# Two scatters in place of one for the last token tile of a two-tile slot

## The chip, the cores and the metric

The kernel runs on one core of a Trainium2 chip. The metric is the device time of one execution in microseconds (us): the median of several runs. The profile shows one execution instruction by instruction. Its engines are PE (TensorE: matmuls), DVE (VectorE), ACT (ScalarE), POOL (GpSimd, which also issues the indirect DMAs) and SP (SyncE, which issues the plain loads).

## The reference

Attention with a soft cap on the scores is followed by a mixture of experts in which every token goes to exactly one of eight experts. The change lies in the second part, and there in the line that writes `out[mask]`.

```python
def _moe_ref(x, modality_id, w_gate, modality_bias, w1, w2):
    # x (3584, 768), w1 (8, 768, 1024), w2 (8, 1024, 768)
    logits = x @ w_gate + modality_bias[modality_id]
    e_idx = np.argmax(logits, axis=1)
    ...
    for e in range(E):
        mask = e_idx == e
        h = np.maximum(x[mask] @ w1[e], 0.0)
        out[mask] = gate_w[mask, None] * (h @ w2[e])
```

## The kernel before, in words

The tokens of an expert are worked on in slots of up to 384 rows, that is three token tiles of 128 rows (`TW = 3`). A plan that the kernel makes on the chip says which expert and which rows each slot has. Eight full slots run first. Then a branch picks one of four ends (`ENDS`, L57 of the program) by the plan; on this input it is the first, `(2, 2, 0)`: a slot of two tiles, a second slot of two tiles, and up to 32 left-over rows of one expert ("few"), whose matmuls are placed among those of the second two-tile slot. Below, "slot A" and "slot B" are these two slots and "few" is the third part.

A slot is `run_slot`: `ffn1` makes the hidden layer, with matmuls of L1103, L1104 and L1107 into `ph`, a relu on ACT (`hh`, L1113) and the rest of the split on DVE (`hl`, L1114). `ffn2` makes the output. For each token tile `t` it runs 48 matmuls of L1139 into two PSUM tiles `py`, one for each half of the 768 columns; tile 0 mixes the two halves, every later tile finishes half 0 before it starts half 1. ACT scales each finished half by the gate weight into the SBUF tile `ot` (L1144), and when both are there POOL issues one indirect DMA (L1145) that scatters 128 rows of 3072 bytes to `out` by the row numbers in `mt`. Few has an `ot` of its own, `of` (L1268), and a scatter of its own (L1269) of 128 rows of 768 bytes, since four quarters of a row lie on four groups of partitions.

Weights come as FP32 through SP loads (L107) into four `raw` buffers, shared in turn; ACT casts each to its high part (L990, `ah`, `bh`), DVE subtracts to get the low part (L991, `al`, `bl`), and with that the buffer is free for the load four places on. The rows of x for the next slot are gathered by POOL (L970), scaled and transposed on DVE.

The order on each engine is that of the program as the scheduler leaves it; every engine works through its queue in order, so an instruction that waits holds up those behind it. Waits are put in where two instructions touch the same tile or tensor. Each scatter of the tiles writes the tensor `out`, so each waits for the landing of the one before it, unless the two are declared independent, which only few's scatter was. The line L1306 is the branch that leaves an end, L1554 the close of the program, where all engines meet.

Of the kernel before, what the change touches and what calls it, by code (L numbers as in the profile page):

```python
# [42 lines left out]
I32 = mybir.dt.int32  # L43
AF = mybir.ActivationFunctionType
ALU = mybir.AluOpType
# [7 lines left out]
NT, DM, FF, E, NM = B * S, H * D, 1024, 8, 2  # L53
# [8 lines left out]
TW = W // 128  # L62
# [23 lines left out]
class Program:  # L86
# [8 lines left out]
    def pin(self, inst):  # L95
        return self.tc.keep_in_program_order(inst)
# [243 lines left out]
    def slots(self, pool, ps, early):  # L340
# [78 lines left out]
        if early:  # L419
            pair = tile("pair", [128, E])  # L420
            V.scalar_tensor_tensor(pair, rem, 128.0, sm, op0=ALU.is_gt, op1=ALU.mult)
            two = tile("two", [128, 1])
            V.tensor_reduce(two, pair, axis=AX.X, op=ALU.add)
            V.tensor_scalar(two, two, NB, float(FIXED + 2), op0=ALU.add, op1=ALU.is_le)
            first = tile("first1", [128, 1])
            V.scalar_tensor_tensor(first, NB, float(FIXED), two, op0=ALU.is_le, op1=ALU.mult)
            other = tile("other", [128, 1])
            V.scalar_tensor_tensor(other, NB, float(FIXED + 1), two, op0=ALU.is_le, op1=ALU.mult)
            V.tensor_tensor(other, other, first, op=ALU.subtract)
            V.tensor_scalar(begin, total, float(FIXED + 2), 2.0, op0=ALU.is_gt, op1=ALU.add)  # L430
            V.tensor_tensor(begin, begin, other, op=ALU.mult)
            V.tensor_tensor(end, begin, other, op=ALU.add)
            V.scalar_tensor_tensor(end, first, 2.0, end, op0=ALU.mult, op1=ALU.add)
            few = tile("few", [128, 1])
            V.scalar_tensor_tensor(pair, rem, float(FEW), sm, op0=ALU.is_gt, op1=ALU.mult)
            V.tensor_reduce(few, pair, axis=AX.X, op=ALU.add)
            V.tensor_scalar(few, few, NB, float(FIXED + 2), op0=ALU.add, op1=ALU.is_le)
            V.tensor_tensor(few, few, first, op=ALU.mult)
            V.tensor_tensor(end, end, few, op=ALU.subtract)
            V.scalar_tensor_tensor(begin, first, 3.0, begin, op0=ALU.mult, op1=ALU.add)  # L440

            fits = tile("fits", [128, 1])
            V.tensor_scalar(fits, begin, float(FIXED), total, op0=ALU.add, op1=ALU.is_ge)
            V.tensor_tensor(end, end, fits, op=ALU.mult)
            V.memset(begin, float(FIXED))
        else:
            V.memset(plan[:, 1:], 0.0)
# [673 lines left out]
    def ffn2(self, mt, n, at={}, pin=lambda inst: inst):  # L1121

        nc = self.nc
        for t in range(n):
            ot = self.lp.tile([128, C * 256], F32, name="ot", tag="late", bufs=3)[:, :DM]
            rows = slice(t * 128, (t + 1) * 128)
            steps = [[(half, f, a, c) for f in range(FC) for a, c in ((0, 0), (0, 1), (1, 0))] for half in range(2)]
            if t == 0:
                late = [(0, f, 0, 1) for f in range(FC - 3, FC)]
                steps = [[step for step in steps[0] if step not in late] + steps[1][:9] + late, steps[1][9:]]  # L1130
            py, left = [None, None], [3 * FC, 3 * FC]
            for half, f, a, c in steps[0] + steps[1]:
                if a == c == 0 and (2 * t + half, f) in at:
                    at[2 * t + half, f]()
                if py[half] is None:
                    py[half] = self.ps_y.tile([128, 512], F32, name="py")
                cs = slice(half * HALF, (half + 1) * HALF)
                left[half] -= 1
                self.latest["tensor"] = nc.tensor.matmul(  # L1139
                    py[half][:, :HALF], self.h[a][:, f, rows], self.w2s[f][c][:, cs],  # L1140
                    start=left[half] == 3 * FC - 1, stop=left[half] == 0,
                ).ins
                if left[half] == 0:
                    self.latest["scalar"] = pin(nc.scalar.mul(ot[:, cs], py[half][:, :HALF], mt[:, t, 1:2])).ins  # L1144
            self.last_out = nc.gpsimd.indirect_dma_start(  # L1145
                self.out, bass.IndirectOffsetOnAxis(ap=mt.bitcast(I32)[:, t, 0:1], axis=0), ot, None,
                bounds_check=NT - 1, oob_is_err=False,
            )
            self.latest["gpsimd"] = self.last_out.ins

    def run_slot(self, cur, n, ahead=None, between=(), mark=None):
# [111 lines left out]
    def run_few(self, e, rows):  # L1263

        nc, (mt, index) = self.nc, rows
        self.few2(e, (2, 3, 4, 5), True)
        ot = self.small_tile("of")[:, :QC]
        nc.scalar.mul(ot, self.yf[:, :QC], mt[:, 1:2])  # L1268
        put = nc.gpsimd.indirect_dma_start(  # L1269
            self.out.rearrange("n (g d) -> (n g) d", g=4), bass.IndirectOffsetOnAxis(ap=index[:, 0:1], axis=0), ot, None,  # L1270
            bounds_check=4 * NT - 1, oob_is_err=False,
        )
        self.tc.declare_no_dep(put.ins, self.last_out.ins, reason="every token is in one slot of the plan")

    def run_slots(self, cur, order, table):

# [33 lines left out]

    def end(self, end, at, ahead):

        self.last_sp = None
        tiles = ENDS[end]
        for i, n in enumerate(tiles):
            later = (lambda: ahead(FIXED + i + 1, tiles[i + 1])) if i + 1 < len(tiles) else None
            if n:
                at = self.run_slot(at, n, later)
            else:
                self.run_few(*at[:2])  # L1320

    def finish(self, which, end, cur, ahead):

        tc = self.tc
        if end == len(ENDS):
            self.tail()
            return
        with tc.If(which == end + 1, preferred_fallthrough_block=False) as branch:
            self.end(end, cur, ahead)
        with branch.Else():  # L1330
            self.finish(which, end + 1, cur, ahead)
# [122 lines left out]
    def build(self):  # L1454
        tc, nc = self.tc, self.nc
        with ExitStack() as st:
            self.nstage, self.latest = 2, {}
            self.cpool = st.enter_context(tc.tile_pool(name="cpool", bufs=1))
            dram = st.enter_context(tc.tile_pool(name="dram", bufs=1, space=DRAM))
            self.plani = self.cpool.tile([1, 3], I32, name="plani")  # L1460
            with ExitStack() as sa:
                self.up = sa.enter_context(tc.tile_pool(name="up", bufs=1))
                first = self.first = self.load_kq(0, parts=2)
                with tc.tile_pool(name="ps_w", bufs=1, space=PSUM) as ps_w:
                    self.constants(self.cpool, dram)
                    self.warm(ps_w, 13, 256)
                big = nc.values_load(self.flag[0:1, 0:1], min_val=0, max_val=1)
                with tc.If(big != 0, preferred_fallthrough_block=False) as branch:
                    self.general()
                    self.tail(fresh=True)  # L1470
                with branch.Else():
                    with ExitStack() as sb:
                        self.moe_pools(sb)
                        self.small = "xT1"
                        rt = sb.enter_context(tc.tile_pool(name="rt", bufs=1))
                        early, late = self.attention(first, rt)
                        self.moe_pools2(sb)

                        table = []

                        def order():
                            table.append(self.slots(rt, self.ps_r, True))
                            self.meta = next(table[0])

                        w2 = lambda at, *ks: (at, lambda: self.load_w2(early[0], self.raws, range(*ks)))
                        self.run_slots(early, (
                            *late, (3, order), w2(3, 0, 4), *(w2(f, f, f + 1) for f in range(4, FC)),
                        ), table)
# [70 lines left out]
```

## Time and profile before

| | |
|---|---|
| median of 3 runs | 801.45 us (801.19 to 802.93) |
| profiled execution, its own time | 802.65 us |
| its span, first to last instruction | 800.80 us |
| PE busy | 791.1 us, 99% of the span |
| DVE, ACT, POOL busy | 555.2, 513.0, 306.5 us |
| scatters of tiles, L1145 | 28, mean 1137 ns on POOL |

The page gives busy times and shares over the whole span. PE is busy for 99% of it, so what there is to read are PE's few gaps and the time behind its last matmul. A row of the timeline has the start in us, the length in us, the engine, the line, the operation and its tiles, with the count at its end (several instructions in a row are merged), and in brackets how long the engine had been idle before it and what released it. A letter q behind an engine (POOLq, SPq) is its queue: waits, moves, DMA issues and the closing of the program. The view of stretches has the busy time of each engine in each stretch, then the granted clock as a share, the mean busy share of the 16 DMA engines and the GB/s moved. In the view of the DMA queues q1 carries the loads of SP and q0 the DMAs of POOL.

### The profile page before, as it was taken

Reading aid. Unit: us, or ns where it says so; the run is one execution under the profiler, and the core shown is the slowest. Engines: PE = TensorE matmul, PEld = TensorE weight load, DVE = VectorE, ACT = ScalarE, POOL = GpSimd, SP = SyncE. Lnnn points to the kernel's source line nnn. Section 1 sums busy time; section 2 is a strip of 40 time slices with the busy share of each in tenths; the row PEclk is TensorE's granted clock in tenths of the full one; section 3 lists DMA queues with packets and bytes.
Section 4 is the critical chain, followed back from the end, with each engine's and each line's share of the span. In section 5 each row is a group of like instructions: output and inputs, shape, how many; then the busy total and the mean of one; then the engine's idle time right before and its main releaser. Section 6 shows DMA issues by size and latency. Waiting matters only on the chain. (4 is left out here: it accounts for less than half of the span.)

```text
span 800.8 us, 14596 instructions
## 1 busy us (share of the span) xinstructions
PE 791.1 (99%) x5272; PEld 624.2 (78%) x5272; DVE 555.2 (69%) x1086; ACT 513.0 (64%) x598; POOL 306.5 (38%) x382
## 2 busy tenths in 40 slices
PE   8999999999999999999999999999999999999997
PEld 4444454444445445999999999999999999999986
DVE  6889898999999999966383753737437374356820
ACT  7999999999999998365252542535425354245611
POOL 2122423232324145457565273542745417014201
PEclk9999999999999999999999999999999999999999
DMA  6475464746556444497366382563825638248654
GB/s 214 148 237 193 146 192 125 212 149 197 173 167 204 137 155 151 112 338 245 106 202 233 108 278 84 182 231 112 275 76 179 229 112 265 70 141 263 204 219 166
DMA packets 55939, 144.77 MB, mean 181 GB/s; under 512 B 11567, under 2 KB 19585, under 8 KB 55858
## 3 DMA queue, kind: packets, MB, share of 16 engines
q1 hardware_dynamic: 40960, 109.42, 41.0%
q0 software_dynamic: 14752, 34.33, 14.1%
q8 instruction: 43, 0.70, 0.4%
q14 instruction: 38, 0.31, 0.1%
q10 hardware_dynamic: 146, 0.00, 0.0%
HBM read 114.91 MB, written 24.34 MB: 174 GB/s over the span
## 5 line engine op out<-in xcount | busy, mean ns | idle before, releaser
L1103 PE MATMUL ph<-x,ah 128*128 128x384 f32 (+1 forms) x480 | 156.5, 326 | 1.3 <-DVE hl L1114 1.3
L1104 PE MATMUL ph<-x,ah 128*128 128x384 f32 (+1 forms) x480 | 155.9, 325 | 0.0
L1107 PE MATMUL ph<-x,al 128*128 128x384 f32 (+1 forms) x480 | 155.9, 325 | 0.0
L1139 PE MATMUL py<-bh,hl 128*128 128x384 f32 x448 | 149.9, 335 | 0.9 <-DVE hl L1114 0.9
L1139 PE MATMUL py<-bh,hh 128*128 128x384 f32 x448 | 150.3, 336 | 0.0
L1139 PE MATMUL py<-bl,hh 128*128 128x384 f32 x448 | 146.5, 334 | 0.0
L970 POOL DMA_INDIRECT xg<-xd,at x93 | 116.2, 1249 | 50.4 <-issue 23.5
L702 POOL DMA_DIRECT2D xd<-xs x96 | 61.2, 645 | 174.4 <-DVE xs L696 170.0
L557 ACT ACTIVATE pt<-sc,isc 128x896 f32<-128x896 f32 x129 | 120.6, 1009 | 5.7 <-PE sc L553 2.9
L991 DVE TENSOR_TENSOR bl<-raw,bh 128x768 fp32r<-128x768 f32 x80 | 74.3, 956 | 70.5 <-ACT bh L990 56.6
L560 ACT ACTIVATE pt<-pt,cabs 128x2688 f32<-128x2688 f32 x48 | 122.0, 2541 | 0.8
L602 PE MATMUL xT<-pt,va 128*64 128x448 f32 x576 | 118.8, 548 | 1.1 <-ACT pt L560 1.1
L1113 ACT ACTIVATE hh<-ph 128x384 fp32r<-128x384 f32 (+1 forms) x80 | 37.3, 469 | 124.5 <-PE ph L1107 119.7
L1114 DVE SCALAR_TENSOR_TENSOR hl<-ph,hh 128x384 fp32r<-128x384 f32 (+1 forms) x80 | 41.8, 527 | 105.9 <-ACT hh L1113 105.8
L1103 PEld LDWEIGHTS ph<-x,ah 128*128 128x128 f32 x480 | 90.1, 188 | 1.7 <-DVE hl L1114 1.7
L1145 POOL DMA_INDIRECT out_dram<-ot,mt x28 | 31.8, 1137 | 152.4 <-ACT ot L1144 141.2
L1104 PEld LDWEIGHTS ph<-x,ah 128*128 128x128 f32 x480 | 90.1, 188 | 0.0
L1107 PEld LDWEIGHTS ph<-x,al 128*128 128x128 f32 x480 | 90.1, 188 | 0.0
L990 ACT CAST bh<-raw 128x768 fp32r<-128x768 f32 x80 | 64.3, 834 | 32.3 <-DMA raw<-in_w_dram 25.6
L1139 PEld LDWEIGHTS py<-bh,hl 128*128 128x128 f32 x448 | 84.1, 188 | 1.2 <-DVE hl L1114 1.2
L1139 PEld LDWEIGHTS py<-bh,hh 128*128 128x128 f32 x448 | 84.1, 188 | 1.2 <-issue 0.7
L1139 PEld LDWEIGHTS py<-bl,hh 128*128 128x128 f32 x448 | 83.8, 188 | 0.0
(217 smaller groups left out, 1307.3 us busy)
## 6 DMA issues: line engine op xcount, KB each, us to landing
raw<-in_w_dram SPq DMA_DIRECT2D x86, 384.0 KB, 4.0
raw<-in_w_dram SPq DMA_DIRECT2D x60, 512.0 KB, 5.3
kq<-in_kq_dram SPq DMA_DIRECT2D x47, 448.0 KB, 4.6
va<-in_v_dram SPq DMA_DIRECT2D x24, 448.0 KB, 6.1
xd<-xs POOLq DMA_DIRECT2D x96, 112.0 KB, 3.8
cg<-gl SPq DMA_DIRECT2D x22, 224.0 KB, 2.2
raw<-in_w_dram SPq DMA_DIRECT2D x12, 256.0 KB, 3.8
mapd<-pre SPq DMA_DIRECT2D x4, 480.0 KB, 5.2
```

Source lines behind the costliest of these rows:

```text
L557: pin(nc.scalar.activation(out, sc[:, :, :S], AF.Tanh, scale=scale))
L560: pin(nc.scalar.activation(x, x, AF.Exp, scale=self.cabs))
L602: pin(pe.matmul(xT[j * D : (j + 1) * D, :S], va[:, u * D : (u + 1) * D], quads[q]["pt"][t, i][:, j], start=t == i == 0, stop=t == 1 and i ...
L702: (nc.gpsimd.dma_start(self.xd[b * S : (b + 1) * S, a, r * 64 : (r + 1) * 64].rearrange("(n p) f -> p n f", p=32), d["out"][a * 32 : (a + ...
L970: got = self.nc.gpsimd.indirect_dma_start(self.xg[:, c], None, self.xd.rearrange("n a x -> (n a) x"), bass.IndirectOffsetOnAxis(ap=at[:, c ...
L990: a = self.nc.scalar.copy(hi, raw)
L991: b = self.nc.vector.tensor_tensor(lo, raw, hi, op=ALU.subtract)
L1103: nc.tensor.matmul(ph[:, :w], hi[:, fs], self.x[k][:, 0, :w], start=first, stop=False)
L1104: nc.tensor.matmul(ph[:, :w], hi[:, fs], self.x[k][:, 1, :w], start=False, stop=False)
L1107: nc.tensor.matmul(ph[:, :w], lo[:, fs], self.x[k][:, 0, :w], start=False, stop=last)
L1114: self.latest["vector"] = nc.vector.scalar_tensor_tensor(hl[:, f, :w], acc, 0.0, hh[:, f, :w], op0=ALU.max, op1=ALU.subtract).ins
L1139: self.latest["tensor"] = nc.tensor.matmul(py[half][:, :HALF], self.h[a][:, f, rows], self.w2s[f][c][:, cs], start=left[half] == 3 * FC - ...
```

## The change

In `ffn2`, the last tile of a slot with fewer than three tiles (`n < TW and t == n - 1`) is written by two scatters of 128 rows of 1536 bytes, one for each half of the columns. `out` is seen for this as a tensor with twice as many rows of half the length, so each half needs row numbers of its own, 2 x row and 2 x row + 1: POOL makes them with two small `tensor_scalar` into a tile `twice`, of which there is one buffer. All other tiles keep one scatter. The scatters of an end are collected in `self.puts` and each is declared independent of those before it in the same end.

```diff
@@ ffn2
             rows = slice(t * 128, (t + 1) * 128)
+            where, parts = mt.bitcast(I32)[:, t, 0:1], 1
+            if n < TW and t == n - 1:
+                parts = 2
+                both = self.lp.tile([128, parts], I32, name="twice")
+                for h in range(parts):
+                    nc.gpsimd.tensor_scalar(both[:, h : h + 1], where, float(parts), float(h), op0=ALU.mult, op1=ALU.add)
+                where = both
...
-            self.last_out = nc.gpsimd.indirect_dma_start(
-                self.out, bass.IndirectOffsetOnAxis(ap=mt.bitcast(I32)[:, t, 0:1], axis=0), ot, None,
-                bounds_check=NT - 1, oob_is_err=False,
-            )
+            for h in range(parts):
+                self.last_out = nc.gpsimd.indirect_dma_start(
+                    self.out.rearrange("n (h d) -> (n h) d", h=parts),
+                    bass.IndirectOffsetOnAxis(ap=where[:, h : h + 1], axis=0),
+                    ot[:, h * DM // parts : (h + 1) * DM // parts], None, bounds_check=parts * NT - 1, oob_is_err=False,
+                )
+                self.scattered(self.last_out)
@@ run_few
-        self.tc.declare_no_dep(put.ins, self.last_out.ins, reason="every token is in one slot of the plan")
+        self.scattered(put)
+
+    def scattered(self, put):
+
+        for other in self.puts or ():
+            self.tc.declare_no_dep(put.ins, other.ins, reason="every token is in one slot of the plan, and the halves have columns of their own")
+        if self.puts is not None:
+            self.puts.append(put)
@@ end
-        self.last_sp = None
+        self.last_sp, self.puts = None, []
```

PE, DVE and SP keep their instructions, their order and their waits. What moves is on POOL, and one wait on ACT.

POOL, from the last gathers of the end `(2, 2, 0)` to its branch, before. DMASW0 to DMASW7 are the eight semaphores that POOL's DMAs use in turn, DVE, Activation and Pool those of the engines:

```order
L970 DMA xg<-xd,at_9981 128x192 [waits DMASW2_49,DVE_49]
L1145 DMA out_dram<-ot,mt 3584x768 [waits DMASW3_49,Activation_49]
L1145 DMA out_dram<-ot,mt 3584x768 [waits DMASW4_49,DMASW3_49,Activation_49]
L1145 DMA out_dram<-ot,mt 3584x768 [waits DMASW5_49,DMASW4_49,Activation_49]
L1145 DMA out_dram<-ot,mt 3584x768 [waits DMASW6_49,DMASW5_49,Activation_49]
L1269 DMA out_dram<-of,index 14336x192 [waits DMASW7_49,Activation_49]
L1306 UNCONDITIONAL_BRANCH [waits Pool_49,Pool_sequencer_49]
```

The same stretch with the change:

```order
L1132 TENSOR_SCALAR twice<-mt 128x1 x2
L970 DMA xg<-xd,at_9981 128x192 [waits DMASW2_49,DVE_49]
L1153 DMA out_dram<-ot,mt 3584x768 [waits DMASW3_49,Activation_49]
L1153 DMA out_dram<-ot,twice 7168x384 [waits DMASW4_49,Activation_49,Pool_49]
L1153 DMA out_dram<-ot,twice 7168x384 [waits DMASW5_49,Activation_49,Pool_49]
L1132 TENSOR_SCALAR twice<-mt 128x1 [waits DMASW5_49,DMASW4_49]
L1132 TENSOR_SCALAR twice<-mt 128x1
L1153 DMA out_dram<-ot,mt 3584x768 [waits DMASW6_49,Activation_49]
L1153 DMA out_dram<-ot,twice 7168x384 [waits DMASW7_49,Activation_49,Pool_49]
L1153 DMA out_dram<-ot,twice 7168x384 [waits DMASW0_49,Activation_49,Pool_49]
L1279 DMA out_dram<-of,index 14336x192 [waits DMASW1_49,Activation_49]
L1323 UNCONDITIONAL_BRANCH [waits Pool_sequencer_49]
```

The scatters of tile 1 of slot A and of slot B are now pairs. The waits for the scatter before are gone; what stays of DMASW is each DMA's own semaphore, from eight DMAs back. In a pair the wait for ACT is no longer the last of the waits, since one for POOL's own row numbers follows it. The row numbers of slot A are made ahead of few's gather, those of slot B behind slot A's pair, for whose landings they wait.

ACT, the last part of slot B, before (`hs` and `of` belong to few):

```order
L1144 ACTIVATE ot<-py,mt 128x384 [waits DMASW3_49,PE_49,Activation_49]
L1240 ACTIVATE hs<-ph 128x256 [waits PE_49]
L1144 ACTIVATE ot<-py,mt 128x384 [waits DMASW4_49,PE_49,Activation_49]
L1268 ACTIVATE of<-ptr,mf 128x192 [waits DMASW5_49,DVE_49,PE_49]
```

With the change:

```order
L1151 ACTIVATE ot<-py,mt 128x384 [waits DMASW3_49,PE_49,Activation_49]
L1250 ACTIVATE hs<-ph 128x256 [waits PE_49]
L1151 ACTIVATE ot<-py,mt 128x384 [waits DMASW4_49,DMASW5_49,PE_49,Activation_49]
L1278 ACTIVATE of<-ptr,mf 128x192 [waits DVE_49,PE_49]
```

Half 0 of slot B's tile 1 takes the buffer of slot A's tile 1 and so waits for two landings instead of one; `of` has one wait fewer.

## Rows read from the trace of the kernel before

**Rows 1.** Head of the profile's page

```profile
span 800.8 us, 14596 instructions
```

**Rows 2.** Timeline, from the last matmuls on, all engines

```profile
794.38 1.51 PE L1256 MATMUL ptr<-raw,hf 128*32 128x192 f32 x32
795.34 0.98 POOL L1145 DMA_INDIRECT out_dram<-ot,mt  x1 [10.57 <-ACT ot L1144]
795.95 0.42 ACT L1268 ACTIVATE of<-ptr,mf 128x192 f32<-128x192 f32 x1 [0.89 <-PE ptr L1256]
796.65 0.98 POOL L1269 DMA_INDIRECT out_dram<-of,index  x1 [0.33 <-POOLq L1306]
```

**Rows 3.** Instructions of L1554 from 785 us on (ns min/median/max, first and last start)

```profile
L1554 POOLq DRAIN  x3: 46/115/3374, 796.6 to 800.5; - x3
L1554 SPq DRAIN  x3: 7/7/12, 799.5 to 800.2; - x3
```

**Rows 4.** Waits of SP's queue from 770 us on: total us, times, longest

```profile
SPq L1554 <- DMA out_dram<-of,index: 0.5, 1, 0.5
```

**Rows 5.** Stretches behind the last matmul

```profile
796.80:798.00 1.20, 0.00 (x0) 0.00 (x0) 0.00 (x0) 0.00 (x0) 0.83 (x1) 1.00 0.78 312
798.00:798.20 0.20, 0.00 (x0) 0.00 (x0) 0.00 (x0) 0.00 (x0) 0.00 (x0) 1.00 0.00 0
```

**Rows 6.** Timeline of POOL: a gather among eight, slots A and B

```profile
728.19 1.00 POOL L970 DMA_INDIRECT xg<-xd,at  x1 [0.30 <-DMA out_dram<-ot,mt]
...
749.90 1.80 POOL L1145 DMA_INDIRECT out_dram<-ot,mt  x1 [0.30 <-ACT ah L990]
758.34 1.11 POOL L1145 DMA_INDIRECT out_dram<-ot,mt  x1 [6.64 <-ACT ot L1144]
783.78 0.98 POOL L1145 DMA_INDIRECT out_dram<-ot,mt  x1 [24.34 <-ACT ot L1144]
```

**Rows 7.** Instructions of L1306 (ns min/median/max, first and last start)

```profile
L1306 POOLq EVENT_SEMAPHORE  x2: 17/17/17, 796.4 to 796.5; - x2
```

**Rows 8.** Timeline of ACT, slot A's tile 1 and the last weights of slot B

```profile
750.38 0.58 ACT L1144 ACTIVATE ot<-py,mt 128x384 f32<-128x384 f32 x1
...
756.74 0.83 ACT L990 CAST bh<-raw 128x768 fp32r<-128x768 f32 x1 [1.04 <-PE ph L1103]
757.48 0.58 ACT L1144 ACTIVATE ot<-py,mt 128x384 f32<-128x384 f32 x1
...
763.03 0.84 ACT L990 CAST bh<-raw 128x768 fp32r<-128x768 f32 x1 [1.85 <-DMA raw<-in_w_dram]
```

**Rows 9.** Timeline of DVE and PE at PE's gap in slot B

```profile
763.91 0.96 DVE L991 TENSOR_TENSOR bl<-raw,bh 128x768 fp32r<-128x768 f32 x1 [1.68 <-ACT bh L990]
...
765.91 0.39 PE L1103 MATMUL ph<-x,ah 128*128 128x256 f32 x1 [1.26 <-DVE hl L1114]
```

**Rows 10.** DMA queues from 753.5 to 755.5 us: packets, MB, share

```profile
q1 hardware_dynamic: 156, 0.42, 55.3%
q0 software_dynamic: 79, 0.38, 45.8%
```

**Rows 11.** DMA queues from 761 to 762 us

```profile
q0 software_dynamic: 56, 0.34, 81.6%
q1 hardware_dynamic: 39, 0.07, 20.4%
```

**Rows 12.** Timeline of SP's queue, the last weight load of slot B

```profile
758.60 0.33 SPq L107 DMA_DIRECT2D raw<-in_w_dram  x1
```

**Rows 13.** Timeline of ACT, half 0 of slot B's tile 1

```profile
788.71 0.58 ACT L1144 ACTIVATE ot<-py,mt 128x384 f32<-128x384 f32 x1 [4.22 <-PE py L1139]
```

**Rows 14.** Stretch behind few's last weight loads

```profile
793.10:794.40 1.30, 1.30 (x12) 1.05 (x10) 0.00 (x0) 0.00 (x0) 0.00 (x0) 1.00 0.09 29
```

**Rows 15.** Groups of POOL by line: busy us, mean ns

```profile
L950 POOL TENSOR_SCALAR index<-mf,quarter 128x1 int32<-128x1 int32 x1 | 1.9, 1857 | 1.3 <-DMA mf<-mapd 1.3
```

More of the change, by code (lines that the diff above doesn't have):

```diff
@@ L1325, in finish @@
         if end == len(ENDS):
+            self.puts = None
             self.tail()
@@ L1456, in build @@
         with ExitStack() as st:
-            self.nstage, self.latest = 2, {}
+            self.nstage, self.latest, self.puts = 2, {}, None
             self.cpool = st.enter_context(tc.tile_pool(name="cpool", bufs=1))
```

## Prediction

> **What bounds the kernel now.** I read the head of the page first, then the end of the timeline, then the gaps of PE in the last two slots, since nothing ahead of the end `(2, 2, 0)` is touched. The span is 800.80 us [rows 1] and the execution's own time 802.65 us, so 1.85 us lie around the span; I leave them as they are.
>
> The end. PE's last work is few's product, 794.38 to 795.89 [rows 2]. The scatter of slot B's tile 1 starts at 795.34, released by ACT's `ot`; ACT makes `of` from 795.95 to 796.37, and few's scatter starts at 796.65, 0.28 us behind it [rows 2]. The reader should see how close two limits lie there: a gather in an unbroken series is 1.00 us long with 0.30 us idle before it [rows 6], so POOL starts an indirect DMA every 1.30 us, and few's starts 1.31 us behind the tile's. It could not have started more than about 0.01 us sooner, whichever limit one takes away. What closes the program is POOL's drain: it starts at 796.6, lasts 3.37 us and so ends at 799.97 [rows 3], while SP, which waits for the landings, is at its own drain at 799.5 [rows 3]; its wait for few's landing is 0.5 us [rows 4]. So POOL's own work on few's scatter is last, about 0.45 us behind all landings.
>
> PE's gap. In slot B, PE is idle for 1.26 us before 765.91, waiting for DVE's `hl` [rows 9]. DVE was late since it works in order and stood 1.68 us before 763.91 for the last `bl` [rows 9], whose `bh` ACT could start only at 763.03, after 1.85 us of waiting for a load [rows 8]. That load was issued at 758.60 [rows 12]. Between 761 and 762 the queue of POOL's DMAs, which is the scatter of slot A's tile 1 issued at 758.34 [rows 6], moved 0.34 MB and the loads 0.07 MB [rows 11]. So the tile's 0.39 MB (128 rows of 3072 bytes) stand in the way of the load that makes PE's gap. This is the one place of the end where the change can touch PE.
>
> **The change, part by part.**
>
> *Waits between scatters removed.* Nothing: the tiles' scatters start at 749.90, 758.34, 783.78 and 795.34 [rows 2, 6], 8 us or more apart, and all of these but the first were released by ACT's `ot`, not by a landing. The first stood behind a gather. Few's scatter had no such wait before.
>
> *Row numbers, two pairs on POOL.* The nearest row, the index of few, has 1857 ns for one of this shape [rows 15]; four make 7.4 us at most. The first pair stands before few's gather, in time in which POOL waits for DVE. The second waits for the landings of slot A's pair and delays only slot B's first scatter, at 783.78 and 24.34 us behind the previous one [rows 6]. Without that cover a pair would cost 3.7 us; I take 0.
>
> *ACT's extra wait in slot B.* Half 0 of tile 1 is at 788.71 after 4.22 us idle [rows 13], 30 us behind slot A's last scatter: 0.
>
> *Slot B's tile 1 in two.* The early half can go at about 789.6, behind the `ot` that ends at 789.29 [rows 13]. It adds 0.20 MB to the stretch in which few's last two weight loads arrive; these are through by 793.1, where the DMA share falls to 0.09 [rows 14], and are needed in the second half of few's matmuls, from about 795.1 (half of 1.51 us behind 794.38 [rows 2]). A whole tile takes 0.94 us of the DMA engines (0.78 of 1.20 us [rows 5]), half a tile 0.47 us, against about 2 us of slack: 0; if the slack were gone, at most 0.47. The late half is issued where the whole tile was, and moves 0.47 us less. That gains nothing: between 798.0 and 798.2 no DMA runs at all [rows 5], so few's transfer did not stand behind the tile's bytes but came when POOL was ready with it. Its wait moves, though. The three waits of the late half end in POOL's own row numbers, so that ACT's release is now taken by an instruction ahead of the DMA. Two such queue instructions in a row start 0.1 us apart [rows 7]. The late half starts 0 to 0.1 us later, and few's scatter, which must keep 1.30 us behind it and has 0.01 us to spare, and then the drain, follow. I take +0.08.
>
> *Slot A's tile 1 in two.* Here both signs meet. Half 0 is ready at 750.96 [rows 8], while POOL is in tile 0's scatter until 751.70 [rows 6]; the early half is issued at about 752.0. The whole tile, issued at 758.34, moved its bytes after 761, 2.7 us later; so the early half moves from about 754.7 on. There the loads need the DMA too: from 753.5 to 755.5 they moved 0.42 MB beside 0.38 MB of a scatter [rows 10], some 0.40 MB in each us and no room left. One of the loads in flight is the one whose `bh` starts at 756.74, and behind it in ACT's order stands the tile's second `ot` at 757.48 [rows 8]; the buffer that it fills is the one that the load of 758.60 waits for. So a delay of that load moves the last load and the late half alike. With the shares of [rows 10] the early half displaces about its own size in loads at half rate, 0.24 us; the bounds are 0 (if it comes between two loads) and 0.47. On the other side the late half displaces only half of what the tile did. By [rows 11], where the scatter had 82% of the DMA time, that gives back 0.8 x 0.47 = 0.39 us to the last load, with bounds 0 and 0.47. Together -0.15 us, bounds -0.47 and +0.47; PE's gap of 1.26 us goes to about 1.1, and what follows on PE has no gap as large, so the end moves with it.
>
> By the Trainium skill (page "DMA: Bandwidth & Descriptors", section "Queues, rings and completion order"), a DMA engine takes turns between the queues with work, one packet at a time, so that a scatter could not hold back a load for long. The trace does not agree in either stretch: 56 packets against 39 [rows 11] and 79 against 156 [rows 10]. With turns of equal packets the saving of the late half would be nearer 0.24 us, and the sum of this edit about 0 instead of -0.15.
>
> *Sum.* -0.15 + 0.08 = -0.07 us, from 802.65 to about 802.6 for the profiled execution. That execution was 1.2 us above the median of the runs, 801.45; on that scale the change gives **801.4 us**.
>
> **The rivals.** A change under 0.2%, 1.6 us here, is about what a measurement of this kernel cannot tell from none.
>
> *The late half gives back everything, the early half is free.* PE's gap shrinks by 0.47 us, with +0.08 at the end: 801.05 us. If, against [rows 3], the drain waited for the last tile's bytes, another 0.47 us would go: 800.6 us. For it speaks the 82% of [rows 11], against it the full DMA around 755 [rows 10]. Even so the sum stays inside the 1.6 us.
>
> *Slower: the early half collides with slot B's weights.* Place: the loads in flight around 755. The load of `bh` at 756.74 lands up to 0.47 us later; with it the last load is issued later, and if the late half then still meets it, nothing is given back. PE's gap grows to 1.7 us: 801.45 + 0.47 + 0.08 = 802.0 us. It decides the sign as soon as the early half delays that load by more than the late half returns (0.39). To be slower by over 0.2% it would have to cost three times its own transfer, for which I see no row.
>
> *The change does nothing that the time shows.* Both halves fall where they cost and give the same: 801.45 us; this is the neighbour of my forecast and the same verdict.
>
> **How the numbers follow.** My forecast, within 0.25 us of 801.4, has 0.50; the first rival 0.22, the second 0.20; 0.08 is left for something else in the end, such as the fetch of POOL's longer program. The range takes both bounds, 800.9 and 802.0, and the spread of three runs, 801.19 to 802.93, of which the upper side is wider: 800.5 to 802.5. Only the remainder and the far ends of the rivals reach 1.6 us: faster 0.04, slower 0.06, same 0.90.
>
> **What would show it.** Pairs of scatters at about 752 and 758 to 759, and 789.6 and 795.4; few's scatter about 1.30 us behind the last half, its drain still about 3.3 us long and ending last; a gap of PE near 764.7 between 0.8 and 1.7 us, with the same releaser; no gap of PE in few's product at 794.4. I am wrong if the drain ends together with the landing of the last half, if PE's gap is gone or above 2 us, or if POOL's row numbers stand between ACT's `ot` and a scatter.

## The result and the profile after

The changed kernel took 807.12 us (median of 6 runs, 806.81 to 809.52) where the kernel before took 801.69 us beside it (6 runs, 800.47 to 803.98). The ratio is 1.0062, with a 95% interval of 1.0047 to 1.0076: slower by 0.6%, or 3.8 to 6.1 us. The prediction had 801.4 us, a range of 800.5 to 802.5, and 0.06 for slower. It was wrong.

The profiled execution of after took 806.81 us, and that of before 802.65. The head of its page, beside [rows 1]:

```profile
span 805.2 us, 14605 instructions
```

The first thing to see is where the two executions part. I compared the start of each PE instruction with that of its counterpart; the change leaves PE the same instructions in the same order. Below, a product is one matmul, a stretch is a run of products of one kind, and the spacing is the time from the start of one product to the start of the next. Here are two rows of PE's timeline of before, in slot 2: the first product of the first projection (L1103), and the first product of its second projection (L1139 before, L1146 after), 144 products later.

```profile
419.42 0.34 PE L1103 MATMUL ph<-x,ah 128*128 128x384 f32 x1
...
444.37 0.34 PE L1139 MATMUL py<-bh,hh 128*128 128x384 f32 x1
```

The same two products after:

```profile
420.17 0.34 PE L1103 MATMUL ph<-x,ah 128*128 128x384 f32 x1
...
445.61 0.33 PE L1146 MATMUL py<-bh,hh 128*128 128x384 f32 x1
```

Before, 144 products take 24.95 us, 173.3 ns each; after, 25.44 us, 176.7 ns each. PE waits for nothing in either stretch. This happens in all seven full slots 1 to 7 (in before 173.33 ns throughout, in after 176.69) and in the first projection alone; the second runs at 173.3 to 173.4 ns in both. The change has no instruction there. The difference of the two spans, by stretches between the same PE instructions of both traces:

| stretch | before, us | after, us | difference |
|---|---|---|---|
| up to slot 1's first product | 369.49 | 369.77 | +0.28 |
| slots 1 to 7 | 349.48 | 352.80 | +3.32 |
| slot A, first projection | 17.13 | 16.80 | -0.33 |
| slot A, second projection | 17.83 | 19.30 | +1.47 |
| slot B, first projection | 18.39 | 17.55 | -0.84 |
| slot B, second projection, few's first parts | 22.06 | 21.95 | -0.11 |
| few's last product to few's scatter | 2.27 | 2.75 | +0.48 |
| few's scatter to the end of the span | 4.15 | 4.24 | +0.09 |

The sum is +4.36 us. More than four fifths of it lie ahead of the end that the change is about, most of it in slots 1 to 7. The 0.28 us of the first row are of the run: in a second trace of the kernel before (below) slot 1's first product starts at 369.76 us.

In slots A and B the gaps of PE changed places. PE's gap in slot A before:

```profile
740.61 0.45 PE L1139 MATMUL py<-bh,hl 128*128 128x384 f32 x1 [0.88 <-DVE hl L1114]
```

Rows of PE and DVE after, as in [rows 9]:

```profile
744.28 0.69 DVE L1047 TENSOR_TENSOR xg<-xg,rec 128x512 f32<-128x512 f32 x1 [3.46 <-DMA xg<-xd,at]
...
745.36 0.44 PE L1146 MATMUL py<-bh,hl 128*128 128x384 f32 x1 [2.36 <-DVE hl L1114]
...
765.35 0.38 PE L1103 MATMUL ph<-x,ah 128*128 128x256 f32 x1 [0.22 <-DVE hl L1114]
...
769.74 0.39 PE L1103 MATMUL ph<-x,ah 128*128 128x256 f32 x1
```

The gap of 1.26 us in slot B that the prediction was about stood ahead of the first product of the sixth of eight groups. After, that product is the one at 769.74, and less than 0.1 us is left there; a gap of 0.22 us stands two groups earlier, at 765.35. But PE stands 2.36 us in slot A, where it stood 0.88 us before, since DVE waits for the gathered rows of slot B. POOL's timeline, beside [rows 6], has the second of the eight gathers at 1.73 us:

```profile
729.16 1.73 POOL L970 DMA_INDIRECT xg<-xd,at  x1 [0.31 <-issue]
...
738.97 0.35 POOL L1132 TENSOR_SCALAR twice<-mt 128x1 int32<-128x1 int32 x2
...
756.74 1.68 POOL L1153 DMA_INDIRECT out_dram<-ot,twice  x1 [0.31 <-ACT bh L990]
763.98 0.98 POOL L1153 DMA_INDIRECT out_dram<-ot,twice  x1 [5.55 <-issue]
769.25 0.34 POOL L1132 TENSOR_SCALAR twice<-mt 128x1 int32<-128x1 int32 x2 [4.29 <-DMA out_dram<-ot,twice]
...
793.86 0.99 POOL L1153 DMA_INDIRECT out_dram<-ot,twice  x1 [5.15 <-ACT ot L1151]
```

The pairs of halves stand at 756.74 and 763.98 (slot A) and at 793.86 and 799.63 (slot B); less the 3.6 us by which slot A begins later, they are within about 1.5 us of their forecast places. The pairs of row numbers take 0.35 us and hold up no scatter. ACT's last `ot` before, whose scatter is the one at 795.34 in [rows 2]:

```profile
794.48 0.58 ACT L1144 ACTIVATE ot<-py,mt 128x384 f32<-128x384 f32 x1 [5.19 <-PE py L1139]
```

The end after, beside [rows 2]:

```profile
798.17 1.51 PE L1266 MATMUL ptr<-raw,hf 128*32 128x192 f32 x32
798.27 0.58 ACT L1151 ACTIVATE ot<-py,mt 128x384 f32<-128x384 f32 x1 [5.19 <-PE py L1146]
799.63 0.98 POOL L1153 DMA_INDIRECT out_dram<-ot,twice  x1 [4.77 <-issue]
799.74 0.42 ACT L1278 ACTIVATE of<-ptr,mf 128x192 f32<-128x192 f32 x1 [0.89 <-PE ptr L1266]
800.92 0.99 POOL L1279 DMA_INDIRECT out_dram<-of,index  x1 [0.30 <-issue]
```

ACT's `ot` ends at 798.85 and the late half starts at 799.63, 0.78 us behind it; the whole tile before started 0.28 us behind its `ot`, which ended at 795.06. Few's scatter follows 1.29 us behind the late half, as forecast, and so 2.75 us behind the start of few's product, not 2.27. POOL's drain, 4.0 us long since it begins ahead of few's scatter, ends 3.4 us behind the start of that scatter; before it was 3.3. The instructions of L1153 from 790 us on show why the late half is late:

```profile
L1153 POOLq EVENT_SEMAPHORE  x2: 5179/5386/5592, 787.5 to 793.7; - x2
L1153 POOL DMA_INDIRECT out_dram<-ot,twice x2: 985/990/995, 793.9 to 799.6; - x2
```

The wait that starts at 793.72 (793.7 in the row) and lasts 5179 ns ends at 798.90, 0.04 us behind `ot`: ACT's release is taken here, ahead of the scatter, and the scatter starts 0.73 us behind that.

The trace of before holds the same delay, in a scatter of a full slot that waits for ACT itself and for no row numbers. There it is a landing that comes last, and an instruction ahead of the scatter takes it:

```profile
L1145 POOLq EVENT_SEMAPHORE  x1: 10974/10974/10974, 620.8 to 620.8; - x1
...
632.54 1.03 POOL L1145 DMA_INDIRECT out_dram<-ot,mt  x1 [2.80 <-ACT hh L1113]
```

The wait of 10974 ns ends at 631.77 and the scatter starts 0.77 us behind that.

### The profile page after: what moved, and what is told of

Same layout as the page of the kernel before. It is cut to its first block, busy times and chain, and to the rows that moved or that the text cites. A ratio compares the mean times of both kernels' runs of the same rounds, so it can differ in the third digit from the quotient of the medians.

```text
span 805.2 us, 14605 instructions
## 1 busy us (share of the span) xinstructions
PE 794.0 (99%) x5272; PEld 627.5 (78%) x5272; DVE 554.7 (69%) x1086; ACT 512.8 (64%) x598; POOL 310.9 (39%) x388
## 5 line engine op out<-in xcount | busy, mean ns | idle before, releaser
L1103 PE MATMUL ph<-x,ah 128*128 128x384 f32 (+1 forms) x480 | 157.3, 328 | 0.2 <-DVE hl L1114 0.2
L1146 PE MATMUL py<-bh,hl 128*128 128x384 f32 x448 | 149.9, 335 | 2.4 <-DVE hl L1114 2.4
L1146 PE MATMUL py<-bh,hh 128*128 128x384 f32 x448 | 150.3, 336 | 0.0
L1146 PE MATMUL py<-bl,hh 128*128 128x384 f32 x448 | 146.5, 334 | 0.0
L1103 PEld LDWEIGHTS ph<-x,ah 128*128 128x128 f32 x480 | 90.1, 188 | 0.5 <-DVE hl L1114 0.4
L1146 PEld LDWEIGHTS py<-bh,hl 128*128 128x128 f32 x448 | 84.1, 188 | 2.7 <-DVE hl L1114 2.7
L1146 PEld LDWEIGHTS py<-bh,hh 128*128 128x128 f32 x448 | 84.1, 188 | 1.2 <-issue 0.7
L1146 PEld LDWEIGHTS py<-bl,hh 128*128 128x128 f32 x448 | 83.8, 188 | 0.0
L1153 POOL DMA_INDIRECT out_dram<-ot,mt x26 | 30.7, 1181 | 135.2 <-ACT ot L1151 122.2
```

What stands on the lines that cost most here:

```text
L1103: nc.tensor.matmul(ph[:, :w], hi[:, fs], self.x[k][:, 0, :w], start=first, stop=False)
L1146: self.latest["tensor"] = nc.tensor.matmul(py[half][:, :HALF], self.h[a][:, f, rows], self.w2s[f][c][:, cs], start=left[half] == 3 * FC - ...
```

## The experiments

The first question was what makes products slower that the change doesn't touch. The compiled programs have one difference that reaches them. The tile `twice` takes 32 bytes of each partition, and every tile allocated behind it stands 32 bytes further on. Of the operands of the products in slots 1 to 7 these are `bh` and `bl` (the moving operand of the second projection) and `hh` and `hl` (its stationary one). The operands of the first projection, `x`, `ah` and `al`, have not moved. Tiles of the attention and the routing moved as well; none of them is an operand of a product in slots 1 to 7.

The runs below were made beside many runs of the kernel before, on chips on which single times spread by 0.5 to 1.5%. A plain copy of the kernel before, among them, came out at 0.9986 with an interval of 0.9975 to 0.9998; so a ratio alone tells nothing under 0.2% here, and the traces have to.

**Only the place.** The kernel before, and this at the place of the row numbers:

```diff
+            if n < TW and t == n - 1:
+                self.lp.tile([128, 2], I32, name="twice")
```

> The kernel before, with one tile that nothing writes or reads, 8 bytes a partition, at the place in pool lp where the change allocates its row numbers. It takes 32 bytes, and the tiles allocated behind it (bh and bl, hh and hl, and others) move up by 32 bytes, as in the changed kernel; no instruction is added. Theory A (the addresses): the products of L1103, L1104 and L1107 of the seven full slots 1 to 7 start 176.7 ns apart as in the changed kernel, not 173.3 as before; 144 x 7 x 3.4 ns = 3.4 us, so 804.9 to 805.5 us. Theory B (the scatters, the longer program of POOL or where the program lies make the products slower): spacing 173.3 ns and 801.3 to 802.1 us.

PE's timeline of this kernel, slot 1 (first product of either projection):

```profile
370.07 0.34 PE L1103 MATMUL ph<-x,ah 128*128 128x384 f32 x1
...
395.51 0.33 PE L1141 MATMUL py<-bh,hh 128*128 128x384 f32 x1
```

25.44 us, 176.7 ns a product, and a ratio of 1.0045 (1.0018 to 1.0072). This is theory A: a tile that nobody uses costs what the change costs in slots 1 to 7.

**The change without the place.** The changed kernel, its tile in a pool that is opened last:

```diff
+        self.last = pool("last", 1)
...
-                both = self.lp.tile([128, parts], I32, name="twice")
+                both = self.last.tile([128, parts], I32, name="twice")
```

> The changed kernel, with its tile of row numbers in a pool of its own that is opened last, so that no other tile has another address than before. Theory A: spacing 173.3 ns in slots 1 to 7, so 3.4 us of the loss are gone: 807.1 - 3.4 = 803.7 us, and if what is different in the end (the gap of PE in slot A's second projection, 2.4 us against 0.9, and the smaller one in slot B) hangs on the addresses too, 801.4 to 802.4. Theory B: 176.7 ns and 806.5 to 807.5 us as in the changed kernel.

```profile
370.24 0.34 PE L1104 MATMUL ph<-x,ah 128*128 128x384 f32 x1
...
395.20 0.34 PE L1147 MATMUL py<-bh,hh 128*128 128x384 f32 x1
```

24.96 us, 173.3 ns; the ratio is 1.0002 (0.9978 to 1.0026). The time of its profiled run, 805.29 us, doesn't compare with 802.65, being from another chip. The late half starts 0.78 us behind `ot` here too.

**The same tile, 64 bytes; and the declarations alone.** In the changed kernel:

```diff
-                both = self.lp.tile([128, parts], I32, name="twice")
+                both = self.lp.tile([128, 16], I32, name="twice")[:, :parts]
```

> The changed kernel, with the tile of row numbers 64 bytes long, so that the tiles behind it move by 64 bytes and not by 32. Theory A, where only the address modulo 64 counts: spacing 173.3 ns and the time of the run with the tile behind all others, 801.4 to 803.7 us. Theory A, where every shift counts: 176.7 ns and 805 to 807 us. Theory B: 176.7 ns, 806.5 to 807.5 us.

176.6 ns and 1.0043 (1.0018 to 1.0068): a shift by 64 bytes is as slow as one by 32. Without the split (`parts = 1` for every tile):

> The changed kernel without its split: every tile is written by one scatter, no row numbers are made, no tile is added and none moves; only the scatters of an end are declared independent of one another. Theory A: 173.3 ns and 801.3 to 802.1 us, as before. Theory B, if the declarations are to blame: 176.7 ns, 805 us or more; if the split's instructions are, as theory A.

173.3 ns and 1.0011 (0.9989 to 1.0034): the declarations cost nothing that shows.

**A state, or the tiles themselves?** The changed kernel with its addresses as they are, and a product more at the head of each full slot:

```diff
+                if first and f == 0 and n == TW:
+                    nc.tensor.matmul(ph[:, :64], hi[:, fs], self.x[k][:, 0, :64], start=True, stop=True)
```

> The changed kernel, its addresses as they are, with one product of 64 columns more at the head of each full slot's first projection (its result is written over by the product behind it). Theory C (the slow spacing is a state of TensorE's pipeline that the last products of the slot before leave behind, and a disturbance can end it): the spacing in slots 1 to 7 is no longer 176.7 ns throughout but 173.3 or another value; at 173.3 the time is 3.4 us less and 7 or 8 small products of some 0.05 us more, so about 804 us where the changed kernel has 807.1. Theory D (what is written to or read from the moved tiles during these products slows each of them): 176.7 ns and about 0.4 us longer than the changed kernel, 807.5.

PE's timeline, slot 2: the small product, the first two of the 144, and the head of the second projection.

```profile
419.84 0.19 PE L1103 MATMUL ph<-x,ah 128*128 128x64 f32 x1
419.87 0.42 PE L1105 MATMUL ph<-x,ah 128*128 128x384 f32 x1
420.13 0.33 PE L1106 MATMUL ph<-x,ah 128*128 128x384 f32 x1
...
444.92 0.34 PE L1148 MATMUL py<-bh,hh 128*128 128x384 f32 x1
```

From 420.13 on, 143 products take 24.79 us, 173.4 ns. The stretch is 25.08 us with the small product, against 25.44 without. The ratio is 1.0003 (0.9988 to 1.0018). One disturbance at the head ends the slow spacing for the whole stretch, with every tile where it was slow. That is theory C and not D: in slots 1 to 7 TensorE keeps one of two spacings through a stretch, and a disturbance can change it.

The same can be read in three traces where PE stood still inside a slot. The plainest is in the kernel with row numbers from DVE (below), whose tiles all stand as before. In its slot 2 PE lost several us, with a mean granted clock of 0.80 (for 3.4 us the lower level, 1.2 GHz, was granted); the rows are the first product, the nineteenth (just ahead of it), the thirty-fourth (behind it) and the last.

```profile
420.53 0.34 PE L1104 MATMUL ph<-x,ah 128*128 128x384 f32 x1
...
423.65 0.34 PE L1104 MATMUL ph<-x,ah 128*128 128x384 f32 x1
...
431.27 0.34 PE L1104 MATMUL ph<-x,ah 128*128 128x384 f32 x1
...
450.71 0.34 PE L1108 MATMUL ph<-x,al 128*128 128x384 f32 x1
```

Ahead of the stall it is 3.12 us for 18 products, 173.3 ns; behind it 19.44 us for 110, 176.7 ns, at a granted clock of 1.00. The next slot ran at 173.3 ns again. In the 64-byte kernel a stall in slot 2, with 1.00 granted throughout, did the opposite: 176.5 ns ahead of it, 173.4 behind. The third is slot 7 of the kernel with 128 unused bytes (below). A stall need not change the spacing: in slot 2 of the kernel with the unused tile of 32 bytes it was 176.7 ns ahead of one and 176.6 behind, and three other stalls in the two kernels with row numbers from DVE left the fast spacing as it was.

**Whose place?** The kernel before, with 32 bytes between `bl` and `hh`:

```diff
         self.w2s = [[wp.tile([128, DM], F32R, name=f"b{h}{k}") for h in "hl"] for k in range(FC)]
+        wp.tile([128, 8], F32, name="gap")
         self.h = [wp.tile([128, FC, W], F32R, name=f"h{h}") for h in "hl"]
```

> The kernel before, with 32 unused bytes between the weight tiles bh and bl of the second projection and the tiles hh and hl, so that of all tiles only hh and hl move. If the place of hh and hl sets the spacing of the first projection (the second projection loads its stationary operand from them): 176.7 ns in slots 1 to 7 and 3.4 us more than before. If it takes the place of bh and bl as well: 173.3 ns and the time of before.

```profile
419.58 0.33 PE L1104 MATMUL ph<-x,ah 128*128 128x384 f32 x1
...
444.54 0.34 PE L1140 MATMUL py<-bh,hh 128*128 128x384 f32 x1
```

24.96 us, 173.3 ns, ratio 0.9999 (0.9986 to 1.0013): in slots 1 to 7 `hh` and `hl` may move. Slot 0 gained. These are the 74th and the last of the 144 products of its first projection, before and then with the gap:

```profile
329.99 0.34 PE L1104 MATMUL ph<-x,ah 128*128 128x384 f32 x1
...
342.36 0.34 PE L1107 MATMUL ph<-x,al 128*128 128x384 f32 x1
```

```profile
330.09 0.34 PE L1105 MATMUL ph<-x,ah 128*128 128x384 f32 x1
...
342.23 0.34 PE L1108 MATMUL ph<-x,al 128*128 128x384 f32 x1
```

70 spacings in 12.37 us are 176.7 ns, in 12.14 us 173.4: the same two spacings, and the kernel before already has the slow one here. (The expectation of the last run below has 177.8 and 174.6 for this: means over 72 products with one spacing of some 0.26 us at their head.) In slot 0 the place of `hh` and `hl` does bear on it. With the same gap in the changed kernel:

> The changed kernel with 32 unused bytes between bl and hh: bh and bl stand 32 bytes behind their place in the kernel before, as in the changed kernel, hh and hl 64 bytes. If the slow spacing comes with the place of bh and bl alone: 176.7 ns in slots 1 to 7 and the time of the changed kernel. If it takes both kinds of tiles in certain places (the entry from the second projection into the next first one decides, and it depends on both): 173.3 ns is as likely, and 3.4 us less.

```profile
421.16 0.34 PE L1104 MATMUL ph<-x,ah 128*128 128x384 f32 x1
...
446.60 0.34 PE L1147 MATMUL py<-bh,hh 128*128 128x384 f32 x1
```

25.44 us, 176.6 ns, ratio 1.0028 (1.0001 to 1.0054). And the kernel before with an unused tile of 128 bytes in place of 8:

> The kernel before with an unused tile of 128 bytes at the place of the row numbers, so that the tiles behind it move by 128 bytes. If the places count modulo 128 bytes: 173.3 ns in slots 1 to 7 and the time of before. If every shift of both kinds of tiles is slow: 176.7 ns and 3.4 us more, 805 us where before has 801.7.

176.7 ns in slots 1 to 6 and at the head of slot 7, until a stall ended it; ratio 1.0036 (0.9995 to 1.0076). All together, the spacing being that of slots without a stall:

| kernel | `bh`, `bl` moved by | `hh`, `hl` by | spacing, ns | ratio to before |
|---|---|---|---|---|
| before | 0 | 0 | 173.3 | 1 |
| the change | 32 | 32 | 176.7 | 1.0062 |
| unused tile | 32 | 32 | 176.7 | 1.0045 |
| 64-byte row numbers | 64 | 64 | 176.6 | 1.0043 |
| gap before `hh`, changed kernel | 32 | 64 | 176.6 | 1.0028 |
| unused tile of 128 bytes | 128 | 128 | 176.7 | 1.0036 |
| row numbers behind all | 0 | 0 | 173.3 | 1.0002 |
| gap before `hh`, kernel before | 0 | 32 | 173.3 | 0.9999 |

In slots 1 to 7 the spacing goes with the place of `bh` and `bl`, in every trace of these kernels that I have: eight with them in the old place are fast, and the other five without the extra product are slow. A move of `hh` and `hl` alone doesn't make it slow, and no place of theirs that was tried makes it fast again. No run moved `bh` and `bl` alone: `hh` and `hl` moved too in every slow kernel. Slot 0 doesn't follow this rule: behind a small product of another kind it ran at 173.4 ns with the gap in the kernel before and with 64 bytes, and at 176.6 in before, in the change and with 128.

**The late half.** The change with row numbers behind all, split in slot A only:

```diff
-            if n < TW and t == n - 1:
+            if n < TW and t == n - 1 and self.cut:
...
+            self.cut = i == 0
```

> The changed kernel with its row numbers behind all other tiles, and split in slot A only; slot B's tile 1 is one scatter again. Spacing 173.3 ns. If the late half of slot B costs half a microsecond at the end (0.78 us from the end of ACT's ot to its start where the whole tile has 0.28), the tile's scatter starts 0.28 us behind ot and few's scatter 2.27 us behind the start of few's product, not 2.74: 0.48 us less than with both split, that is the time of before, 801.7 us, or a few tenths less if slot A's late half frees the loads. If the 0.5 us is something of the run: 0.78 and 2.74 again.

```profile
795.42 1.51 PE L1267 MATMUL ptr<-raw,hf 128*32 128x192 f32 x32
795.53 0.58 ACT L1152 ACTIVATE ot<-py,mt 128x384 f32<-128x384 f32 x1 [5.19 <-PE py L1147]
796.39 0.99 POOL L1154 DMA_INDIRECT out_dram<-ot,mt  x1 [10.45 <-ACT ot L1152]
797.00 0.42 ACT L1279 ACTIVATE of<-ptr,mf 128x192 f32<-128x192 f32 x1 [0.89 <-PE ptr L1267]
797.69 0.98 POOL L1280 DMA_INDIRECT out_dram<-of,index  x1 [0.32 <-POOLq L1324]
```

The whole tile starts 0.28 us behind `ot`, few's scatter 2.27 us behind the product's start, as before the change; with both slots split and the same addresses it was 2.74. Ratio 0.9996 (0.9982 to 1.0010). Then both split, with the row numbers made by another engine:

```diff
-                both = self.last.tile([128, parts], I32, name="twice")
+                both = self.last.tile([128, parts], I32, name="twice", bufs=2)
-                    nc.gpsimd.tensor_scalar(both[:, h : h + 1], where, float(parts), float(h), op0=ALU.mult, op1=ALU.add)
+                    nc.vector.tensor_scalar(both[:, h : h + 1], where, float(parts), float(h), op0=ALU.mult, op1=ALU.add)
```

> The changed kernel with its row numbers behind all other tiles, in two buffers, and made by DVE instead of POOL, so that the late half waits for no work of POOL's own. If the 0.50 us of the late half is the price of ACT's release standing on a queue instruction ahead of the DMA: the late half starts 0.28 us behind ot, not 0.78, few's scatter 2.27 us behind the start of few's product, not 2.74, and the time is 0.48 us less than with POOL's row numbers, which is the time of before within 0.1%. If the split itself costs it (three scatters for two): 0.78 and 2.74 again. Spacing 173.3 ns.

```profile
804.00 0.58 ACT L1152 ACTIVATE ot<-py,mt 128x384 f32<-128x384 f32 x1 [5.19 <-PE py L1147]
804.86 0.98 POOL L1154 DMA_INDIRECT out_dram<-ot,twice  x1 [4.79 <-ACT ot L1152]
806.21 0.42 ACT L1279 ACTIVATE of<-ptr,mf 128x192 f32<-128x192 f32 x1 [1.63 <-PE ptr L1267]
806.91 0.98 POOL L1280 DMA_INDIRECT out_dram<-of,index  x1 [1.07 <-POOLq L1324]
```

The late half starts 0.28 us behind `ot`: the 0.50 us belong to POOL's own row numbers, which push ACT's release onto the instruction ahead, and not to the split. (The row numbers also have two buffers here, not one; the scatter at 632.54 of before, with no row numbers at all, has the delay too.) The other half of the expectation could not be read, since ACT's `of` came 0.7 us later than in the other traces (1.63 us idle, not 0.89). That is so in five of the runs, with and without the split, and I didn't follow it up. Ratio 0.9990 (0.9965 to 1.0015).

**The kernel before again.**

> The kernel before, once more, for a second trace of it. Every theory: 173.3 ns in slots 1 to 7 and the time of before. What it tells: whether PE's gap in slot A's second projection (1.04 us in the trace of before, 2.5 to 2.9 us in three of the others) and the gaps of slot B go with the program or with the run.

The second of its eight gathers, and PE's gaps in its slots A and B:

```profile
725.78 1.73 POOL L970 DMA_INDIRECT xg<-xd,at  x1 [0.31 <-issue]
...
741.13 0.44 PE L1139 MATMUL py<-bh,hl 128*128 128x384 f32 x1 [1.45 <-DVE hl L1114]
...
765.38 0.38 PE L1103 MATMUL ph<-x,ah 128*128 128x256 f32 x1 [0.16 <-DVE hl L1114]
```

The same program had 0.88 and 1.26 us, at the same products, in the trace that the prediction used. The long gather of 1.73 us, which the changed kernel had in the same place, comes without the change too. The gaps go with the run.

**All put right.** Row numbers from DVE behind all tiles, and the gap before `hh`:

> The split with all that was found put right: row numbers behind all other tiles and made by DVE, and hh and hl 32 bytes further on, where slot 0's 72 products ran at 174.6 ns and not at 177.8. Slots 1 to 7 at 173.3 ns; slot 0 at 174.6, 0.23 us less than before; the late half 0.28 us behind ot. If the split gains nothing of its own: the time of before less 0.2 us, a ratio of 0.9997, which the interval will not tell from 1. If a late half of half the size frees the loads of slot B by as much as the prediction's first rival had it: 0.5 us more, 0.9991.

Slots 1 to 7 at 173.3 ns where no stall fell, slot 0 at 174.6 ns by the mean of the expectation, the late half 0.28 us behind `ot`; ratio 0.9980 (0.9954 to 1.0007). No gain that this can tell from none.

## Why the prediction was wrong

**The step that failed** is the first: that the gaps of PE are to be looked for in the end alone, "since nothing ahead of the end `(2, 2, 0)` is touched". No instruction ahead of it is touched, but the places of tiles are. The row numbers were costed by their instructions (a term of 0, which held: 0.35 us a pair, hidden) and never by their 32 bytes. Those cost 3.3 us in seven slots. A kernel with the bytes and without the change has the slow spacing; the change without the bytes has the fast one and no measurable loss.

**The late half, +0.08.** The mechanism was right, ACT's release taken by an instruction ahead of the scatter, few's scatter held to 1.30 us behind it, and the drain last. The size was off: two queue instructions starting 0.1 us apart were the wrong row. The scatter starts 0.73 us behind the instruction that takes ACT's release, so 0.78 us behind `ot` and not 0.28. It measured +0.50, and +0.48 at few's scatter. The trace of before had a row for it, the scatter at 632.54.

**Slot A's pair, -0.15.** The gap that it was about all but vanished, by more than either bound, and the prediction had named "if PE's gap is gone" as a sign of being wrong. But the kernel before, run again, had 0.16 us there by itself, and the gap ahead of it in slot A was 0.1 us in one of the traces above and 2.9 in another. The first projection of slot B takes 16.8 to 19.0 us in the six traces with one scatter in slot A and 16.8 to 18.5 in the eight with two, so 0.15 us cannot be read from them. The term was read from one execution of something that changes between executions. Whether the early half delays loads or the late half frees them stays open; the net of slots A and B, +0.19 us, says nothing. The packet counts of [rows 10, 11], by which the prediction set turns between the queues aside, don't show whether both queues had work all the time, so they leave that open as well.

**What held.** The removed waits between scatters are worth nothing that shows (1.0011, 0.9989 to 1.0034). Few's scatter is bound by POOL's spacing and the drain closes the program. The split as such, with the bytes out of the way, can't be told from the "nothing" rival: 0.9980 to 1.0002 in four versions, one of them split in slot A only.

Of the 5.0 us of the ratio, 3.3 are shown to be the place of the tiles (that of `bh` and `bl`, as far as the moves above separate them), and 0.5 the late half. The remaining 1.2 us are about half the width of the ratio's interval; no run assigns them.

## What to carry to other kernels

A new tile is an edit to every tile that is allocated behind it. Before its instructions are costed, compare the addresses of the two programs, and put small new tiles behind the large ones; to test a suspicion, add the tile alone. Compare the spacing of unchanged products in the two traces as well, stretch by stretch: 2% there over many slots is more than a change at the end can win. And a gap that rests on when a DMA lands should be read from two executions before a term is made of it.

## What the runs showed of the hardware

The same products, with operands in the same places, no wait and a granted clock of 1.00, run at 173.3 or at 176.7 ns. Through slots 1 to 7 a stretch kept to one of them unless a stall or an extra product came; either spacing followed a stall. Which one a stretch began with went there with the place of the moving operand of the stretch before (one place of four, 32 bytes and more apart, was fast); in slot 0 it changed with the place of the other operand, `hh` and `hl`. Why is not settled: the traces show no cause, and I didn't try other places.

The Trainium skill (page "TensorE: Matmul & The Clock Gate", section "Back-to-back issue gap") gives columns over 2.4 GHz plus 2.5 ns for the isolated gap, by which 384 columns would take an estimated 162.5 ns. Neither spacing here agrees. The page says itself that this is the gap of a product by itself and not of a stream of weight loads and products, as here; for such a stream it gives 81 ns at 128 columns and 131 ns at 512, and both spacings at 384 columns lie above these. It has no second spacing at one clock.

An indirect DMA of POOL that takes ACT's release itself started 0.28 us behind the end of ACT's work (before, and row numbers from DVE). Where an instruction ahead of it took the last release, it started 0.73 us (the late half) and 0.77 us (632.54 in before) behind that instruction's end. The Trainium skill (page "Perfetto Trace Analysis", section "Identifying Dependency Chains") says that an instruction which waits for several engines may get EventSemaphore instructions ahead of it; the row of 5179 ns is one, and its price is not on the page.
